# A gated spectral and token-MLP mixer: row block 0 normalised one row group at a time, its w1 rows loaded alone on both queues, seven w1 column blocks in the first group, and the unfolding of the inverse transform in pairs

## The chip, the cores and the metric

The kernel runs on one core of one Trainium2 chip. The time is device microseconds of one launch. The kernel before took 135.03 us (median of three runs: 133.51, 135.03 and 135.1). Everything else below comes from one profiled execution of it, whose span, from the first to the last instruction, is 132.6 us.

## The reference, cut to what matters

S = 2048 rows (positions), D = 512 columns, F = 1792 hidden units, bf16 in and out.

```
x = A_x                                       # (1, 2048, 512)
g = sigmoid((x * gate_w).sum(-1))             # one gate per row
X = rfft2(x) ; X = X * (w_r + i w_i)          # spectral branch, over both axes
a = irfft2(X)
h = layernorm(x over D)                       # MLP branch, no affine part
u = gelu(h^T w1 + b1)                         # contraction over the 2048 rows -> (D, F)
b = (u w2 + b2)^T                             # back to (2048, D)
out = g * a + (1 - g) * b
```

## The kernel before, in words

**How the work is cut.** Row s of the 2048 is written s = 512 q + 4 p + r: p is the partition (128 of them), q and r run from 0 to 3. A *row block* is one r; it has four *row groups* (q), each 128 x 512. The index j = 4 q + r names one of the 16 tiles of x and of h. The hidden units come in 14 column blocks `ft` of 128.

**The MLP branch.** `m1(ft, j)` (L651-657) is one matmul, 128 x 128 by 128 x 512, that adds tile j of h into the PSUM tile of block ft; 14 x 16 = 224 of them. The first NF = 6 blocks are accumulated side by side, row block after row block, while x still arrives (L659-660); their weights are tile `wa`. The other eight blocks follow one after the other, from two `wb` tiles of four blocks. A block's last matmul is followed by its gelu on ACT (L670). `m2` (L932) is the second MLP matmul, 14 per output tile j, 224 tiles' worth in all, some of the last row tile in three parts.

**The spectral branch** is a hand-made 2-D transform with four matmul stages and butterflies between them. Stage A (`fa`, L513-516) takes a row block of x after a radix-4 step on DVE (`q4a`, `q4b`, L494-501): four groups (dq = 0 to 3) of four matmuls for each r, each group evicted from PSUM by ACT into `X` (L519). Stage B (L621-624) makes `B`, evicted by ACT (L628); then the product with the spectral weights, stage I1 (L838-845), the fold `fq` into the two z tiles (L873-874), and stage I3 (L913-917). I3's result is scaled by the gate on ACT into an `eo` buffer (L923), *unfolded* on DVE (`fold`, L937-941: one copy and four additions or subtractions of 128 x 256), and added to the scaled MLP tile (`fin`, L958). Output tiles 14 and 15 (LATE) are unfolded straight into the output and get the MLP part last (L970).

**Layernorm.** For a group of two j: mean and variance on DVE (`bn`, L462-463), a square root on ACT (`sq`, L472), reciprocal and minus mean over deviation on DVE (`rec`, L476-477), then h, on DVE for j = 0, 8 and 4 (L480) and on ACT for the other 13 (L486).

**PSUM.** Eight banks under three names: `acc` 4, `fa` 2, `fb` 2. Blocks 0 to 3 of the first group accumulate in `acc`, blocks 4 and 5 in `fb`. Stage A uses `fa`, so it has two banks that turn.

**What sets the order.** Nothing is ordered by hand. Each piece of work is a task with an engine, an estimated duration, dependencies, a priority and the pools it takes and gives back (`add`, L149). `Plan.order` (L170-233) plays all tasks through a list scheduler and emits them in the order of its start times; the engines then run their streams in exactly this order and wait where a result is not there. So an estimate that is changed changes the order, and a wait of one instruction holds up all that stand behind it on its engine. Loads go out on the SP queue (L303), some of the first on the ACT queue as well. `wa` and `wb` later hold w2.

**Start of the kernel.** The four x tiles of row block 0 are asked for first, two on each queue; then table `ta` for r = 0 (the moving operand of stage A), and the w1 rows of row block 0 in two loads of 384 KB (L381-383), one on each queue; then x, `ta` and w1 of row blocks 1, 2 and 3 on SP. PE runs 13 warm-up matmuls on zeros (L353).

Of the kernel before, what the change touches and what calls it, by code (L numbers as in the profile page):

```python
# [16 lines left out]
P = 128  # L17
# [5 lines left out]
NW = 7  # L23
# [108 lines left out]

class Task:
# [3 lines left out]
class Plan:  # L137
# [32 lines left out]
    def order(self):  # L170
# [16 lines left out]
        while events:  # L187
# [16 lines left out]
            while progress:  # L204
                progress = False
                for eng, ts in pending.items():
# [15 lines left out]
                    if best.nbytes:  # L222
                        dma_free = max(dma_free, now + best.dur + 1.0) + best.nbytes / 350e3
                        end = dma_free + 0.4
                        clock[eng] = max(clock[eng], dma_free - 5.0)
# [36 lines left out]
def kernel(  # L262
# [25 lines left out]
    NEO, NES = 4, 2  # L288
# [65 lines left out]
    NWARM = 13  # L354
# [4 lines left out]
    add("ACT", 1.5, presq, reads=["eps"], writes=["omg"], prio=-5)  # L359


    for r in range(4):
        if r == 0:
            for q in range(4):
                ld([("x", 0, q)], lambda q=q: t["x"][:, q, 0, :], x4[:, q, 0, :], 131072, -9 + 0.1 * q, "SP" if q < 2 else "ACT")
        else:
            ld([("x", r, q) for q in range(4)], lambda r=r: t["x"][:, :, r, :], x4[:, :, r, :], 524288, 2 * r)
        ld([("ta", r)], lambda r=r: t["ta"][:, r, :], tabs["ta"][:, r, :], 163840, 2 * r + 0.2)

    NF = 6  # L370
# [3 lines left out]
    def ld_w1(r, qs=slice(0, 4), eng=None):  # L374
        def emit():
            if "wa" not in t:
                t["wa"] = sb([P, 4, 4, FA], BF16, "wa")
            dma(t["wa"][:, qs, r, :], w1v[:, qs, r, 0:FA], eng)
        return emit

    for b in range(2):  # L381
        add(("SP", "ACT")[b], 0.5, ld_w1(0, slice(b, 4, 2), (None, A)[b]), writes=[("w1", 0, 4 * b), ("w1", 0, 4 * b + 8)], prio=(0.5, -4)[b],
            alloc=() if b else ["wa"], nbytes=393216, after=[a0])
    for r in range(1, 4):
        add("SP", 0.5, ld_w1(r), writes=[("w1", 0, 4 * q + r) for q in range(4)], prio=2 * r + 0.5, nbytes=786432)
# [8 lines left out]
    def ld_wb(k, q):  # L394
        def emit():
            dma(t["wb", k][:, q], w1v[:, q, :, FA + D * k:FA + D * (k + 1)])
        return emit
# [6 lines left out]
    def load_wb(k, after=(wba, wbb)):  # L404
        for q in range(4):
            add("SP", 0.5, ld_wb(k, q), writes=[("w1", k + 1, 4 * q + r) for r in range(4)], prio=10 + 12 * k + 0.1 * q,
                nbytes=524288, after=after)
# [38 lines left out]
    HACT = set(range(NJ)) - {0, 8, 4}  # L446
    for r in range(4):
        xk = [("x", r, q) for q in range(4)]
        groups = [[0, 2], [1, 3]] if r == 0 else [[0, 1], [2, 3]]
        t["xf", r] = None  # L450
        for b, qs in enumerate(groups):
# [4 lines left out]
            def colv(name, qs=qs, r=r):  # L456
                v = t[name][:].rearrange("p (q r) -> p q r", r=4)
                return v[:, qs[0]:qs[-1] + 1:qs[1] - qs[0], r]

            for j in js:  # L460
# [3 lines left out]
                add("DVE", d1(512) + 0.12, bn, reads=[("x", r, j // 4)], writes=[("mv", j)], prio=1.2 * r - (0.6 if j in (0, 8) else 0))  # L464
            mvk = [("mv", j) for j in js]

            def mvv(c, qs=qs, r=r):
                v = t["mv"][:].rearrange("p (q r) c -> p q r c", r=4)
                return v[:, qs[0]:qs[-1] + 1:qs[1] - qs[0], r, c]
# [13 lines left out]
            add("DVE", 0.25 + 0.32 * len(own), rec, reads=xb + mvk, writes=[("rstd", *g)] + [("h", j) for j in own], prio=1.2 * r - 0.2)  # L483
# [18 lines left out]
        if r == 0:  # L502
            add("DVE", 2 * tt(1024) + 2 * tt(512), lambda: (q4a(0), q4b(0)), reads=xk, writes=[("xf", 0), "st"], prio=-0.5, alloc=["xf"])
# [142 lines left out]
    jorder = [4 * q + r for r in range(4) for q in ((0, 2, 1, 3) if r == 0 else range(4))]  # L646

    def w1of(ft):
        return 0 if ft < NF else 1 + (ft - NF) // 4

    def m1(ft, j):  # L651
        if j == jorder[0]:
            t["u", ft] = ps([P, D], F32, "fb" if 4 <= ft < NF else "acc", 2 if 4 <= ft < NF else 4)
        k = w1of(ft)
        w, c = (t["wa"], ft) if k == 0 else (t["wb", k - 1], (ft - NF) % 4)
# [8 lines left out]
    for n, (ft, j) in enumerate(order):  # L664
        last = j == jorder[-1]
        bank = "fb" if 4 <= ft < NF else "acc"
        m1t.append(add("PE", mm(512), lambda ft=ft, j=j: m1(ft, j), reads=[("w1", w1of(ft), j), ("h", j)], writes=[("u", ft)],
# [209 lines left out]

    for i in range(NW):
        n = (0, 3, 5)
        if i in n:  # L880
            k = n.index(i)

            def w2alloc(k=k):
                t["w2", k] = sb([P, 6, S], BF16, "wa") if k == 0 else sb([P, 4, S], BF16, "wb", 2)
            add("SP", 0.01, w2alloc, writes=[("w2a", k)], prio=31 + i, alloc=["wa" if k == 0 else "wb"])

        def ldw2(i=i):
            w, o = w2at(2 * i)
            dma(w[:, o:o + 2, :], w2v[:, 2 * i:2 * i + 2, :])
        add("SP", 0.5, ldw2, reads=[("w2a", k)], writes=[("w2", i)], prio=31 + i, nbytes=1048576)  # L890

    def w2at(ft):
        k = w1of(ft)
        return t["w2", k], ft - (0, NF, NF + 4)[k]
# [8 lines left out]
    for grp in groups:  # L903
        for j in grp:
# [13 lines left out]
            if j % 2 == 0:  # L918
                add("PE", mm(*[129] * 10), i3, reads=[("z", 0), ("z", 1), "tg"], writes=[("i3", j), ("i3", j + 1)], prio=4, alloc=["fa", "fb"])

            def i3ev(j=j):
                t["eo", j] = sb([P, 2, L], BF16, "eo", NEO)
                A.activation(t["eo", j][:], t["i3", j][:], ActF.Copy, scale=t["g"][:, j:j + 1])  # L923
            add("ACT", act(512, 1), i3ev, reads=[("i3", j), "g"], writes=[("eo", j)], prio=1.5, alloc=["eo"], free=[tag])
            parts = [slice(0, D)] if j < NJ - 1 else [slice(0, L), slice(L, L + P), slice(L + P, D)]
            for n, cs in enumerate(parts):
                for ft in range(NFT):
# [6 lines left out]
                    add("PE", mm(cs.stop - cs.start), m2, reads=[("w2", ft // 2), ("gl", ft)], writes=[("y", j, n)], prio=20 + j + 0.3 * n,  # L934
                        alloc=[("acc", "fa", "fb")[n]] if ft == 0 else (), after=m1t[-16:-15] if ft == 0 else ())
            def fold(e, o, s):
                V.tensor_copy(s[:, :, :, 0], e[:, :, 0:129:128].rearrange("p h k -> p k h"))  # L937
                V.tensor_add(s[:, 0, :, 1:P], e[:, :, 1:P], e[:, :, P + 1:L])
                V.tensor_sub(s[:, 1, :, P - 1:0:-1], e[:, :, 1:P], e[:, :, P + 1:L])
                V.tensor_add(o[:, 0:4:3], s[:, :, 0], s[:, :, 1])  # L940
                V.tensor_sub(o[:, 2:0:-1], s[:, :, 0], s[:, :, 1])
            tfold = tiny(1) + 4 * tt(256)
            quart = lambda v: v.rearrange("p h (k d) -> p (h k) d", k=2)

            if j < LATE:
                def es(j=j, fold=fold, quart=quart):
                    s = sb([P, 2, 2, P], BF16, "es", NES)
                    fold(t["eo", j], quart(t["eo", j][:]), s)
                add("DVE", tfold, es, reads=[], writes=[("eo", j)], prio=4, alloc=["es"], free=["es"])

# [4 lines left out]

                def fin(j=j):
                    o = tbuf(j)
                    V.tensor_add(o, o, t["eo", j][:])  # L958
                add("DVE", tt(512), fin, reads=[("eo", j)], writes=[("o", j)], prio=4, free=["eo"])
            else:  # L960
                def es(j=j, fold=fold, quart=quart):
                    e, s = t["eo", j], sb([P, 2, 2, P], BF16, "es", NES)
                    V.tensor_scalar_add(e[:, 0, 0:129], e[:, 0, 0:129], t["ombb2"][:, j:j + 1])
                    fold(e, quart(tbuf(j)), s)
# [50 lines left out]
```

## Time and profile before

| | |
|---|---|
| median of three runs | 135.03 us |
| lowest, highest | 133.51, 135.1 us |
| span of the profiled execution | 132.6 us |
| PE / DVE / ACT busy in it | 124.6 / 115.3 / 80.5 us |
| moved by DMA | 23.18 MB, mean 175 GB/s |
| first matmul that is not warm-up | 7.71 us |
| last instruction's end on DVE (L970) | 130.09 us |

The page of the profile gives the span of the profiled execution and no launch time of its own; the span is 0.9 us below the lowest of the three runs shown and 2.4 us below their median. A matmul's end in the profile is modelled: a matmul of 512 columns is shown as 380 ns long, though the next starts 216 ns after it, so a PE that is shown busy may still have lost time. "Idle before" is the time for which an engine stood still before an instruction, with what ended it.

### The profile page before, as it was taken

Reading aid. Unit: us, or ns where it says so; the run is one execution under the profiler, and the core shown is the slowest. Engines: PE = TensorE matmul, PEld = TensorE weight load, DVE = VectorE, ACT = ScalarE, POOL = GpSimd, SP = SyncE. Lnnn points to the kernel's source line nnn. Section 1 sums busy time; section 2 is a strip of 40 time slices with the busy share of each in tenths; the row PEclk is TensorE's granted clock in tenths of the full one; section 3 lists DMA queues with packets and bytes.
Section 4 is the critical chain, followed back from the end, with each engine's and each line's share of the span. In section 5 each row is a group of like instructions: output and inputs, shape, how many; then the busy total and the mean of one; then the engine's idle time right before and its main releaser. Section 6 shows DMA issues by size and latency. Waiting matters only on the chain.

```text
span 132.6 us, 2193 instructions
## 1 busy us (share of the span) xinstructions
PE 124.6 (94%) x769; PEld 70.7 (53%) x783; DVE 115.3 (87%) x295; ACT 80.5 (61%) x155; POOL 0.2 (0%) x4
## 2 busy tenths in 40 slices
PE   6749999999999999999999999999999999999991
PEld 2234464545544566744445544556865766655590
DVE  2987999999999997389999999999598599999841
ACT  4036699999999999972222016235994857755200
POOL 0000000000000000000000000000000000000000
PEclk9999999999999999999999999999999999999999
DMA  4899999925499565999964930000000003034031
GB/s 133 245 370 394 393 380 371 321 60 134 90 309 342 96 134 131 337 373 413 421 253 72 420 146 2 0 2 5 0 0 0 5 0 158 23 135 161 2 119 40
DMA packets 17350, 23.18 MB, mean 175 GB/s; under 512 B 1446, under 2 KB 14780, under 8 KB 17340
## 3 DMA queue, kind: packets, MB, share of 16 engines
q1 hardware_dynamic: 16780, 22.39, 49.8%
q10 hardware_dynamic: 560, 0.66, 1.6%
q8 instruction: 6, 0.10, 0.3%
q14 instruction: 4, 0.03, 0.1%
HBM read 20.93 MB, written 2.10 MB: 174 GB/s over the span
## 4 chain that ended last, share of the span: by engine, by line
PE 80%; DVE 10%; DMA 6%; SPq 1%; issue 1%
PE acc L932 35%; PE acc L656 25%; DMA x<-in_A_x_dram 6%; DVE stats L462 4%; PE fb L656 3%; PE fa L838 1%; PE fb L838 1%; PE fa L624 1%; PE fb L624 1%; SPq L303 1%; DVE mv L463 1%; DVE gl L495 1%; DVE st L494 1%; PE fa L513 1%; DVE nmr L477 1%
## 5 line engine op out<-in xcount | busy, mean ns | idle before, releaser
L932 PE MATMUL acc<-gl,wb 128*128 128x512 bf16 (+1 forms) x123 | 30.5, 373 | 0.3
L656 PE MATMUL acc<-h,wb 128*128 128x512 bf16 x124 | 28.8, 379 | 0.2
L932 PE MATMUL acc<-gl,wa 128*128 128x512 bf16 (+1 forms) x94 | 23.2, 372 | 0.1
L932 PEld LDWEIGHTS <-wb 128*128 128x128 bf16 x144 | 14.9, 114 | 10.7 <-DMA wb<-in_B_w_dram 0.6
L952 ACT ACTIVATE x<-acc,ombb,omg 128x512 bf16<-128x512 f32 x14 | 10.7, 778 | 15.5 <-PE acc L932 15.4
L656 PEld LDWEIGHTS <-wb 128*128 128x128 bf16 x128 | 12.4, 97 | 13.5
L656 PE MATMUL acc<-h,wa 128*128 128x512 bf16 x62 | 16.8, 379 | 1.2 <-DVE stats L462 0.7
L932 PEld LDWEIGHTS <-wa 128*128 128x128 bf16 x108 | 11.7, 114 | 8.5
L656 PEld LDWEIGHTS <-wa 128*128 128x128 bf16 x96 | 9.1, 98 | 10.3 <-DMA wa<-in_B_w_dram 0.9
L670 ACT ACTIVATE gl<-acc,b1f 128x512 bf16<-128x512 f32 x12 | 8.5, 708 | 9.6 <-PE acc L656 9.6
L462 DVE BATCH_NORM_STATS2 stats<-x 128x6 f32<-128x512 bf16 x16 | 10.8, 673 | 2.8 <-DMA x<-in_A_x_dram 2.8
L519 ACT CAST X<-fa 128x512 bf16<-128x512 f32 x16 | 8.8, 583 | 3.9 <-PE fa L516 3.8
L486 ACT ACTIVATE h<-x,nmr,rstd 128x512 bf16<-128x512 bf16 x13 | 9.8, 805 | 1.2 <-DVE nmr L477 1.2
L684 ACT ACTIVATE x<-x 128x512 bf16<-128x512 bf16 x16 | 10.2, 672 | 0.0
L923 ACT ACTIVATE eo<-fa,g 128x512 bf16<-128x512 f32 x8 | 5.5, 688 | 6.7 <-DVE x L958 5.0
L656 PE MATMUL fb<-h,wa 128*128 128x512 bf16 x31 | 9.0, 379 | 0.0
L513 PE MATMUL fa<-rot,gl 128*128 128x256 bf16 x16 | 4.3, 272 | 2.1 <-DMA rot<-dft_ta 2.1
L353 PE MATMUL fa<-xp 128*128 128x512 bf16 x13 | 4.4, 514 | 1.2 <-DVE xp L314 1.2
L923 ACT ACTIVATE eo<-fb,g 128x512 bf16<-128x512 f32 x8 | 5.5, 686 | 0.0
L958 DVE TENSOR_TENSOR x<-x,eo 128x512 bf16<-128x512 bf16 x14 | 5.4, 418 | 0.0
L628 ACT CAST B<-fb 128x512 bf16<-128x512 f32 x8 | 5.2, 651 | 0.0
L628 ACT CAST B<-fa 128x512 bf16<-128x512 f32 x8 | 5.1, 639 | 0.0
(170 smaller groups left out, 227.3 us busy)
## 6 DMA issues: line engine op xcount, KB each, us to landing
wb<-in_B_w_dram SPq DMA_DIRECT2D x8, 512.0 KB
wb<-in_B_w_dram SPq DMA_DIRECT2D x4, 1024.0 KB
wa<-in_B_w_dram SPq DMA_DIRECT2D x3, 1024.0 KB
wa<-in_B_w_dram SPq DMA_DIRECT2D x3, 768.0 KB
x<-in_A_x_dram SPq DMA_DIRECT2D x3, 512.0 KB
out_dram<-x SPq DMA_DIRECT2D x3, 512.0 KB
rot<-dft_ti SPq DMA_DIRECT2D x1, 736.5 KB
rot<-dft_ta SPq DMA_DIRECT2D x4, 160.0 KB
```

Source lines behind the costliest of these rows:

```text
L462: V.bn_stats(out=t["stats"][:, j, :], in_=t["x"][:, j // 4, j % 4, :])
L486: add("ACT", act(512, 2), lambda j=j: A.activation(t["h"][:, j // 4, j % 4, :], t["x"][:, j // 4, j % 4, :], ActF.Identity, bias=t["nmr"][ ...
L513: T.matmul(pa[:, 1], lhsT=w(2), rhs=ta[:, 256:512], start=True, stop=False)
L519: add("ACT", act(512), lambda r=r, dq=dq: A.copy(t["X"][:, :, r, :, dq, :], t["pa", r, dq][:]), reads=[("pa", r, dq)], writes=[("X", r, dq ...
L628: A.copy(t["B"][:, lt, e, 2 * c:2 * c + 2, :].rearrange("p s (i b) -> p s i b", b=4), t["pb", lt, e, c][:].rearrange("p s b i -> p s i b"))
L656: T.matmul(t["u", ft][:], lhsT=w[:, j // 4, j % 4, c * P:(c + 1) * P], rhs=t["h"][:, j // 4, j % 4, :], start=(j == jorder[0]), stop=(j == ...
L670: gelus.append(add("ACT", act(512, 1), lambda ft=ft: A.activation(t["gl"][:, ft, :], t["u", ft][:], ActF.Gelu_apprx_tanh, bias=t["b1f"][:, ...
L684: A.activation(t["x"][:, q, r, :], t["x"][:, q, r, :], ActF.Copy, accum_out=t["glog"][:, 4 * q + r:4 * q + r + 1])
L923: A.activation(t["eo", j][:], t["i3", j][:], ActF.Copy, scale=t["g"][:, j:j + 1])
L932: T.matmul(t["y", j, n][:, cs], lhsT=w[:, o, 512 * q + r:512 * q + 512:4], rhs=t["gl"][:, ft, cs], start=(ft == 0), stop=(ft == NFT - 1))
L952: A.activation(tbuf(j).rearrange("p h d -> p (h d)"), t["y", j, 0][:], ActF.Identity, bias=t["ombb2"][:, j:j + 1], scale=t["omg"][:, j:j + 1])
L958: V.tensor_add(o, o, t["eo", j][:])
```

## The change

Four things are changed, and the planner's estimates with them, so that nearly every engine's order moves.

1. *Row block 0.* It is normalised in four groups of one j (order q = 0, 2, 1, 3) in place of two groups of two, `rec` gets an earlier and the radix-4 step a later place on DVE (PQ0 = 1.1 in place of -0.5). The x tiles go out as q = 0, 1 on SP and 2, 3 on ACT as before. Table `ta` for r = 0 now stands behind w1.
2. *First w1 rows.* The rows of q = 0 are asked for directly behind x, the lower 64 partitions on ACT and the upper 64 on SP; then q = 2 and q = 3 on ACT, q = 1 on SP.
3. *Seven column blocks first.* NF is 7: block 6 of the first group accumulates in an `fa` bank. The two `wb` tiles now get four and three blocks. w2 is loaded in 14 loads of 512 KB in place of 7 of 1 MB. Warm-up matmuls: 10 in place of 13.
4. *Unfolding in pairs.* Tiles j and j + 1 share one `eo` buffer (two buffers of a pair in place of four single ones) and are unfolded by one copy and four operations of twice the size; `fin` too runs on a pair.

```diff
-                        dma_free = max(dma_free, now + best.dur + 1.0) + best.nbytes / 350e3
-                        end = dma_free + 0.4
+                        dma_free = max(dma_free, now + best.dur + 1.0) + best.nbytes / RATE(dma_free)
+                        end = dma_free + 0.9
...
+RATE = lambda t: 300e3 if t < 2.6 else 225e3 if t < 5.9 else 380e3
...
-    NEO, NES = 4, 2
+    NEO, NES = 2, 1
...
-    NWARM = 13
+    NWARM = 10
...
-    add("ACT", 1.5, presq, reads=["eps"], writes=["omg"], prio=-5)
+    add("ACT", 0.05, presq, reads=["eps"], writes=["omg"], prio=-5)
+    Q0 = (0, 2, 1, 3)
...
-        ld([("ta", r)], lambda r=r: t["ta"][:, r, :], tabs["ta"][:, r, :], 163840, 2 * r + 0.2)
+        ld([("ta", r)], lambda r=r: t["ta"][:, r, :], tabs["ta"][:, r, :], 163840, 2 * r + 0.2 if r else -3.5)
-    NF = 6
+    NF = 7
+    WB = (0, NF, NF + 4, NFT)
...
-    for b in range(2):
-        add(("SP", "ACT")[b], 0.5, ld_w1(0, slice(b, 4, 2), (None, A)[b]), ...
+    w1_0(0, 0, LO, "ACT", -8)
+    w1_0(1, 0, HI, "SP", -8)
+    w1_0(0, 2, ALL, "ACT", -4)
+    w1_0(0, 1, ALL, "SP", -4)
+    w1_0(0, 3, ALL, "ACT", -3)
...
-        groups = [[0, 2], [1, 3]] if r == 0 else [[0, 1], [2, 3]]
+        groups = [[q] for q in Q0] if r == 0 else [[0, 1], [2, 3]]
...
+    def bankof(ft):
+        return "acc" if ft < 4 or ft >= NF else "fb" if ft < 6 else "fa"
...
-    for i in range(NW):
-        n = (0, 3, 5)
+    for i in range(NFT):
+        if i in WB:
...
-            dma(w[:, o:o + 2, :], w2v[:, 2 * i:2 * i + 2, :])
+            dma(w[:, o, :], w2v[:, i, :])
...
+                    V.tensor_copy(s[:, :, :, :, 0], e[:, :, :, 0:129:128].rearrange("p j h k -> p j k h"))
+                    V.tensor_add(s[:, :, 0, :, 1:P], e[:, :, :, 1:P], e[:, :, :, P + 1:L])
+                    V.tensor_sub(s[:, :, 1, :, P - 1:0:-1], e[:, :, :, 1:P], e[:, :, :, P + 1:L])
+                    V.tensor_add(o[:, :, 0:4:3], s[:, :, :, 0], s[:, :, :, 1])
+                    V.tensor_sub(o[:, :, 2:0:-1], s[:, :, :, 0], s[:, :, :, 1])
...
+                if j % 2:
+                    def fin(j=j):
+                        o = t["tb_"][:, j - 1:j + 1]
+                        V.tensor_add(o, o, t["eo", j // 2][:])
```

The order that results around the start, engine by engine: DVE does `bn` for q = 0 and 2, then `rec` and h of each, `bn` for q = 1 and 3, `rec` and h of q = 1, `rec` of q = 3, the whole radix-4 step of r = 0, and then four `bn` of row block 1 before its first `rec`. ACT does four square roots, h of q = 3, two stage A evictions, a square root, a third eviction, a square root, h of row block 1 for q = 0 and 1, the fourth eviction, and so on, one or two h between two evictions; its gelu table is loaded after the first eviction of row block 3. PE does 18 m1, a stage A group, 3 m1, a group, 3 m1, a group, 3 m1, a group, 8 m1, a group, and goes on so: the 16 groups of stage A stand singly, with 3 to 9 m1 between two of them.

## The prediction

> **What bounds the kernel now.** I read the page first, then the chain of waits, the timelines of PE, ACT and DVE, and the busy times by stretch. The page says that PE is the bound nearly everywhere, with DVE close to it.
>
> ```profile
> PE 124.6 (94%) x769; PEld 70.7 (53%) x783; DVE 115.3 (87%) x295; ACT 80.5 (61%) x155; POOL 0.2 (0%) x4
> PE 80%; DVE 10%; DMA 6%; SPq 1%; issue 1%
> ```
>
> The second line is the chain that ended last: PE for 80%, and before that DVE (the layernorm of x, 10%) and the load of x. Since a shown matmul overlaps the next one, I count PE by issue instead: a run of nine 512-column matmuls starts one every 0.215 us, a stage A group takes 0.33. All matmuls after the warm-up make 118.6 us, before and after the change alike (224 m1, 224 m2 and 22 us of transform). I call *lost* the clock minus the matmul work issued so far. The timeline of PE gives it at five points:
>
> ```profile
> 7.71 0.27 PE L513 MATMUL fa<-rot,gl 128*128 128x256 bf16 x1 [2.06 <-DMA rot<-dft_ta]
> ...
> 29.37 2.10 PE L656 MATMUL acc<-h,wa 128*128 128x512 bf16 x9
> ...
> 35.83 0.38 PE L706 MATMUL fa<-wt,flip 128*128 128x256 bf16 x2
> ...
> 90.62 0.22 PE L842 MATMUL fa<-rot,B 128*128 128x129 bf16 x1
> ...
> 102.92 0.22 PE L913 MATMUL fa<-tg,xp 128*128 128x129 bf16 x1
> ```
>
> 7.7 is lost at the start, 9.9 at 35.83 (work 25.9), 10.5 at 90.62 (80.1), 10.8 at 102.92 (92.1), 10.9 at PE's end, 129.7. So the start costs 7.7 us, the first 28 us another 2.2, all the rest 1.0. From PE's end to the span's it is 2.9, which the change leaves alone. What the start waits for is in the waits and the timelines of DVE and ACT:
>
> ```profile
> PE fa L513 <- DMA rot<-dft_ta: 2.1, 1, 2.1
> DVE stats L462 <- DMA x<-in_A_x_dram: 2.8, 2, 1.6
> ```
> ```profile
> 10.64 0.69 DVE L462 BATCH_NORM_STATS2 stats<-x 128x6 f32<-128x512 bf16 x1 [1.19 <-DMA x<-in_A_x_dram]
> ```
> ```profile
> 10.02 1.13 ACT L519 CAST X<-fa 128x512 bf16<-128x512 f32 x2 [0.71 <-PE fa L516]
> ...
> 26.18 3.12 ACT L486 ACTIVATE h<-x,nmr,rstd 128x512 bf16<-128x512 bf16 x4
> 29.32 1.28 ACT L670 ACT_TABLE_LOAD   x1
> ```
>
> Row block 1 of x is at DVE at 10.64, and DVE has no idle gap from there to 51 us. ACT, too, is full from 24.3 to 45.4 (20.8 of 21.1 us busy).
>
> **The start.** x is asked for as before, so `bn` begins at 3.35. With 0.81 for each `bn` (3.35, 4.17, 4.97), 0.27 for a `rec` (6.84 to 7.11) and 0.37 for an h, h of q = 0 is ready at 5.65, of q = 2 at 6.25, of q = 1 at 8.43, of q = 3 (on ACT) at 9.5; the radix-4 step (1.87, from 4.97 to 6.84) ends at 10.5. The first w1 rows: ahead of and with them are 0.75 MB, moved by 4.8 us in before's half-microsecond stretches; x of row block 0 was usable about 0.5 after its bytes, x of row block 1 about 2.0 after (1.99 MB by 8.65, landed 10.64). Bounds 5.65 (h) and 9.26 (first m1 before), I take 6.3, nearest to these two rows. So 1.4 us of the 7.7 goes.
>
> The clock: 13 warm-ups end at 5.65, seven at 0.43 us and the rest at 0.216; ten end at 5.0. The gap to the first m1 is then 1.3 us. Before it is 2.06, and 256-column matmuls follow it 0.11 apart, full speed: cost 0. The Trainium skill (TensorE: Matmul & The Clock Gate, Part 1) has the clock halved after an idle window of about 3.4 us; by that rule a first m1 after 8.4 would come cold. The trace, whose gap is shorter, cannot show it.
>
> **Row block 1 is what is late next.** x of row block 1 now has 2.13 MB up to its end in both queues together, before 1.99; at 385 GB/s (the 8.0 to 9.5 stretches) it lands 0.35 later, at 11.0. Counted by SP's own bytes alone (1.29 against 1.34 MB) it would be 10.5; a late share gives 11.4. I take 11.0, as both queues' bytes fit the landing before. The Trainium skill says the same (DMA: Bandwidth & Descriptors, Queues, rings and completion order): the queues share the same 16 engines, packet by packet. That speaks against a gain from asking on both queues; the sum does not use it.
>
> DVE now does four `bn` before the first `rec`: 11.0 + 3.24 + 0.35 = 14.55; h on ACT takes 0.80; PE has row block 1 at 15.5. By then it has done row block 0 (28 m1, four A groups) and one m1, 7.4 us of work: lost 8.1. Before it was 9.1 at that amount of work (16.86). So far the change gains 1.0, and an arrival of w1 anywhere between 5.7 and 7 gives the same.
>
> **One bank for stage A.** Block 6 holds one `fa` bank, so each A group waits for the eviction of the one before. In the trace the eviction starts 0.53 us after its group (9.49 and 10.02), lasts 0.55, and PE has the bank 0.05 later: 1.13, of which the group covers 0.33, so 3.7 m1 must lie between and ACT must be free. But ACT has one or two h (0.74 each) and a square root (0.22) between two evictions. Walking the three streams in their order: group 1 of row block 1 waits 0.3, group 2 0.2, in row block 2 groups 0, 1 and 3 wait 0.05, 0.2 and 0.2, the bias 0.2: 1.1 in all. Row block 3's first group comes at 31.65, lost 9.2. The bounds are 0, if ACT is always ahead, and 2.5, if one h more stands before each of the three longest.
>
> **The table load.** ACT's order has the gelu table (1.28) and a gelu (0.6) between row block 3's first two evictions. Eviction 0: 32.2 to 32.7; load to 34.0; gelu to 34.6; eviction 1 to 35.15. PE has five m1 (1.1 us) after its second group, ends them at 34.2 and stands 1.0 us until 35.2. Before, the load lay behind the last h, beside 29 m1. The remaining waits of row block 3, with a gate sum (0.75) ahead of an eviction, are 0.6. The first flip of W comes at 38.95 with 28.1 us of work done: lost 10.9, against 9.9 before. Here the early start is more than eaten. The load and these waits may cost 0 (table earlier, ACT ahead) to 2.5.
>
> **The middle.** ACT then has five gelu, two W evictions and nine gate sums before the first eviction of B: 38.9 + 9.4 = 48.3, before 46.41. The last B eviction moves from 56.6 to about 59.0 and with it DVE's chain: z, ready at 102.68 before, at about 105.1. PE comes to I3 with 94.0 us of work and 11.2 lost: 105.2. So PE still sets the time, by a hair. The 14 w2 loads take seven SP issues more (0.45 each); SP waits 12.8 us for PE there, so nothing; three blocks instead of four behind the last m1 may save the 0.1 lost between 70.3 and 81.4.
>
> **The pairs.** A pair of tiles takes DVE 2.69 us before (106.81 to 109.50). Twice the size, from rows of that shape (128x508 and 128x512 0.42, starts 0.335 apart; 128x1024 0.69, 0.60 apart): 0.08 + 4 x 0.335 + 0.12 + 0.60 = 2.14; eight pairs save 4.4 us of DVE. But only two pair buffers turn: the third and fifth unfolding wait for two evictions (0.57 + 0.69) after a `fin`, less the next `fin`, about 0.8 each; the last one waits about 1.4, the first 0.6 for its second tile. From z to the last unfolding: 22.3, before 22.9. DVE was 1.0 us ahead of PE at tile 14 (125.62 and 126.65), so either way nothing on the path. If the waits vanished: still nothing, PE sets the end; if they doubled, 1 us.
>
> **Sum.** Start -1.4; row block 1 +0.4; bank +1.1 where before lost 0.7; table and row block 3 +1.6 where before lost 0.2; later the same 1.0 as before: lost 11.9 against 10.9. Span 133.6 against 132.6, and on the median of 135.03 about 136.0.
>
> **Rivals.** *The early start is kept.* If ACT is ahead when PE needs it, what was gained by 15.5 us stays, and only before's own later losses (1.8 from 16.86 on) are added: lost 9.4 to 9.9, 1.0 to 1.5 us less, 133.6. For it: ACT has gaps before 16.3 in before. Against it: it has none from 24.3 to 45.4. With x of row block 1 at 10.5 and no wait in row block 3, 2.5 us or more, under 132.5. *The spectral chain sets the end* (slower). ACT's lag at the first B eviction is 1.9 in my sum; from there on each us goes through B, T and z into I3, where PE's order is fixed. With 2 us more (for instance the gate sums in front of row block 3's evictions twice) z is at 107.2, PE waits at I3, 138.0. It decides from z later than 105.2. *Cold clock*: w1 after 8.4, eight m1 at half speed, 1.7 us, and the A groups pushed behind h of row block 1: 137.5. Against it: the first w1 was there by 9.26 with twice the bytes ahead.
>
> **How the numbers follow.** My sum 0.47, early start kept 0.28, spectral chain 0.20, cold clock 0.05. A measurement of this kernel can tell about 2% (2.7 us) from no change. Faster than 132.3 is only the far end of the first rival: 0.08. Slower than 137.7 is most of the second, part of the cold clock and a tail of my sum: 0.18. Within: 0.74. The range 133.2 to 138.0 leaves out about one in ten on each side. As both signs hold much of the chance: the likeliest case alone runs from 135.0 to 137.0.
>
> **What would show it.** The first m1 near 6.3; `stats` of row block 1 near 11.0; row block 1's first m1 near 15.5 with PE idle before it; PE idle before A groups with ACT named as releaser; a gap of 1 us near 34 behind the table load; the first B eviction near 48; DVE waiting for `eo` in the unfolding. I am wrong if PE has no idle time between 16 and 39, or if z comes before 103.

## The result and the profile after

The changed kernel takes 135.88 us (median of four runs: 135.25, 135.73, 136.03, 136.06) where the kernel before took 134.64 in the runs beside it: ratio 1.011, 95% interval 1.0067 to 1.0154. So it is about 1.2 us slower, inside the 2% that were called "within". About 136.0 was forecast. The profiled execution took 135.25 us with a span of 133.1, so it is 0.6 under the median. Below, medians take in all executions of a kernel, while ratios and intervals leave out the few that took over 1.5% longer than its fastest, and the one profile of such an execution (139.29 us, the changed kernel again) is not used.

The lines of before's page about busy time and the chain of waits have these counterparts on the page after:

```profile
PE 125.3 (94%) x766; PEld 70.6 (53%) x780; DVE 112.4 (84%) x252; ACT 80.4 (60%) x157; POOL 0.2 (0%) x4
```
```profile
DVE 53%; PE 26%; ACT 13%; issue 4%; DMA 2%; DVEq 0%; ACTq 0%
```

PE is as busy as it was, but the chain that ended last no longer runs along PE: 53% of it is on DVE. The chain goes to whichever engine came last, so this alone does not say that DVE sets the time. The PE timeline after (columns: start, length, engine and line, operation, shapes, count, idle time before and what ended it) gives the places that the forecast named:

```profile
6.61 1.02 PE L670 MATMUL acc<-h,wa 128*128 128x512 bf16 x4 [1.04 <-DMA wa<-in_B_w_dram]
...
12.82 0.27 PE L524 MATMUL fa<-rot,gl 128*128 128x256 bf16 x1
...
34.67 0.27 PE L524 MATMUL fa<-rot,gl 128*128 128x256 bf16 x1 [0.91 <-ACT X L530]
...
46.30 0.38 PE L720 MATMUL fa<-wt,flip 128*128 128x256 bf16 x2
...
94.77 0.23 PE L856 MATMUL fb<-rot,B 128*128 128x128 bf16 x1 [0.22 <-DVE B L579]
...
105.12 0.22 PE L926 MATMUL fa<-tg,xp 128*128 128x129 bf16 x1
```

PE's first matmul on data starts 1.1 us earlier than before (7.71), and the first m1 2.7 us earlier (9.26). At 34.67 PE stands for ACT: that is the gap behind the table load. The third flip of W, which stood at 49.20 before, comes at 46.30. At 94.77 a matmul of stage I1 waits for a column butterfly of DVE, and at 105.12 I3 starts. The ACT timeline after shows why PE stood at 34.67:

```profile
31.56 0.58 ACT L530 CAST X<-fa 128x512 bf16<-128x512 f32 x1 [1.61 <-PE fa L527]
32.16 1.28 ACT L684 ACT_TABLE_LOAD   x1
33.46 0.69 ACT L684 ACTIVATE gl<-acc,b1f 128x512 bf16<-128x512 f32 x1
34.04 0.58 ACT L530 CAST X<-fa 128x512 bf16<-128x512 f32 x1
```

Between row block 3's first two evictions stand the load and a gelu: 2.48 us from one CAST to the next. PE has one bank, and gets it 0.05 us after the second CAST.

**Where the time went.** The table below adds up, stage by stage, what PE lost. For each matmul this is the time from its start to the next start, less columns/2400 us and 0.002 us; that is the spacing of an undisturbed run (0.216 us for 512 columns, 0.056 for 128). What is left under 0.012 us is not counted, and a gap of exactly one further 512-column matmul is taken for a missing record. The first column is the start of row block 1's first m1, and "rest" the span less this moment. The losses are counted from row block 1's last A group to the first group of stage B, from there to I3, and from I3 to PE's end.

```
                       row block 1's   rest   lost, row blocks   lost in stage   lost
                       first m1               2 and 3 to B       B and to I3     from I3
before                 16.42 (*)      116.2        0.75              0.95         0.04
pairs only             16.3 (*)       116.5        0.75              0.92         0.46
after                  14.88          118.2        2.33              1.17         0.47
  first gelu held      16.97          117.9        2.31              0.88         0.46
  gate sums held       15.92          118.2        2.44              1.00         0.46
  three pair buffers   15.17          118.1        2.33              1.16         0.32
  13 warm-ups          15.82          118.0        2.04              1.18         0.47
  W imaginary first    14.92          118.2        2.45              0.75         0.45
  gelu + gates held    15.69          118.4        2.64              0.95         0.47
  the same, planned    15.33          118.5        2.80              0.94         0.47
(*) the moment at which as much matmul work (7.35 us) was done
```

The start gained 1.5 us in this execution and the rest became 2.0 longer. Of the 2.2 us more that PE lost in the rest, 1.6 lie in row blocks 2 and 3, 0.2 in stage B to I3 and 0.4 from I3 on. The seven profiles whose kernels emit the same start (leaving out 13 warm-ups, moved w1 loads and six column blocks) put row block 1's first m1 between 14.88 and 16.97, median 15.33. So the typical gain is near 1.1 and, with the median rest of 118.2, the net loss near 0.9 by the profiles, where the launches show 1.2 to 1.6; what makes the difference is not shown. The remarkable column is "rest": it stays at 117.9 to 118.5 whichever stall was taken away. It does so because the three losses together hardly fall (3.97 us in the changed kernel, 3.65 to 4.21 in the rows below it): a stall that an edit took from PE came back at another place on PE.

### The profile page after: what moved, and what is told of

Read it like the earlier page. It is cut to its first block, busy times and chain, and to the rows that moved or that the text cites. A ratio compares the mean times of both kernels' runs of the same rounds, so it can differ in the third digit from the quotient of the medians.

```text
span 133.1 us, 2156 instructions
## 1 busy us (share of the span) xinstructions
PE 125.3 (94%) x766; PEld 70.6 (53%) x780; DVE 112.4 (84%) x252; ACT 80.4 (60%) x157; POOL 0.2 (0%) x4
## 4 chain that ended last, share of the span: by engine, by line
DVE 53%; PE 26%; ACT 13%; issue 4%; DMA 2%; DVEq 0%; ACTq 0%
PE acc L966 12%; DVE stats L473 7%; PE acc L670 4%; DVE xp L791 3%; DVE st L791 3%; ACT x L698 3%; ACT eo L937 3%; DVE st L564 3%; DVE mv L474 2%; DMA x<-in_A_x_dram 2%; ACT gl L684 2%; DVE xp L796 2%; DVE xp L563 2%; DVE B L803 2%; DVE xp L797 2%
## 5 line engine op out<-in xcount | busy, mean ns | idle before, releaser
L966 PE MATMUL acc<-gl,wa 128*128 128x512 bf16 (+1 forms) x107 | 26.9, 372 | 0.2
L966 PE MATMUL acc<-gl,wb 128*128 128x512 bf16 (+1 forms) x110 | 27.1, 372 | 0.1
L670 PE MATMUL acc<-h,wb 128*128 128x512 bf16 x108 | 25.7, 379 | 0.2
L966 PEld LDWEIGHTS <-wa 128*128 128x128 bf16 x126 | 13.4, 114 | 9.8 <-issue 0.2
L966 PEld LDWEIGHTS <-wb 128*128 128x128 bf16 x126 | 13.4, 114 | 9.4
L670 PEld LDWEIGHTS <-wb 128*128 128x128 bf16 x112 | 10.9, 98 | 11.7
L670 PEld LDWEIGHTS <-wa 128*128 128x128 bf16 x112 | 10.1, 98 | 10.7 <-DMA wa<-in_B_w_dram 1.8
L530 ACT CAST X<-fa 128x512 bf16<-128x512 f32 x16 | 9.3, 578 | 5.1 <-PE fa L527 5.1
L684 ACT ACTIVATE gl<-acc,b1f 128x512 bf16<-128x512 f32 x11 | 7.6, 694 | 7.8 <-PE acc L670 7.7
L670 PE MATMUL fa<-h,wa 128*128 128x512 bf16 x15 | 5.4, 379 | 0.0
L483 ACT ACTIVATE rstd<-mv,eps 128x2 f32<-128x2 f32 (+1 forms) x10 | 3.0, 295 | 3.4 <-DVE mv L474 2.8
```

The costliest lines, as they stand in the source:

```text
L530: add("ACT", act(512), lambda r=r, dq=dq: A.copy(t["X"][:, :, r, :, dq, :], t["pa", r, dq][:]), reads=[("pa", r, dq)], writes=[("X", r, dq ...
L670: T.matmul(t["u", ft][:], lhsT=w[:, j // 4, j % 4, c * P:(c + 1) * P], rhs=t["h"][:, j // 4, j % 4, :], start=(j == jorder[0]), stop=(j == ...
L684: gelus.append(add("ACT", act(512, 1), lambda ft=ft: A.activation(t["gl"][:, ft, :], t["u", ft][:], ActF.Gelu_apprx_tanh, bias=t["b1f"][:, ...
L966: T.matmul(t["y", j, n][:, cs], lhsT=w[:, o, 512 * q + r:512 * q + 512:4], rhs=t["gl"][:, ft, cs], start=(ft == 0), stop=(ft == NFT - 1))
```

## The experiments

The theory: what the start gains is spent again at the single `fa` bank and the gelu table load in row blocks 2 and 3; without these the gain would be seen. The rivals: ACT's lag at stage B goes through the spectral chain (DVE) to the end; the pairs cost something; the first rows or the cold clock spoil the start. Each run stands beside runs of the kernel before on the same chip (its medians there: 134.40 to 134.66).

### The changed kernel again

No edit.

> The changed kernel unchanged, as the measure for the other kernels of this call. Every theory: 1.011 times the kernel before, and in the trace the same 8.6 us lost (clock minus matmul work) at row block 3's first stage A group, 9.9 at the first flip of W, 10.5 at I1, 11.1 at I3 and about 11.6 at the end of PE.

Measured: 136.23, ratio 1.0114 [1.0073, 1.0156]. The loss is confirmed.

### Pairs alone

The kernel before with the unfolding of the changed kernel and nothing else of it:

```diff
-    NEO, NES = 4, 2
+    NEO, NES = 2, 1
...
+                    o = e if j < LATE else (tbuf(j), t["tb_"][:, j - 1:j + 1])[1]
...
-                    V.tensor_add(o, o, t["eo", j][:])
+                        V.tensor_add(o, o, t["eo", j // 2][:])
```

> The kernel before with nothing but the unfolding in pairs, two pair buffers. Theory 1: DVE is 3 to 4 us less busy, waits for the evictions into the pair buffers appear, and PE sets the end as before: within 0.3 us of the kernel before. Theory C (the pairs cost it): 0.8 to 1.4 us more than the kernel before. If the unfolding had been on the path: 0.5 us or more less.

Measured: 134.56 beside 134.55, ratio 1.0018 [0.9987, 1.005]: no change that can be told. PE loses 0.4 more from I3 on (0.46 for 0.04), the same as in the changed kernel; the interval, which reaches up to 0.7 us, leaves open whether this gets into the time. The larger part of the loss of the whole change lies elsewhere.

### Three pair buffers

```diff
-    NEO, NES = 2, 1
+    NEO, NES = 3, 1
```

> The changed kernel with three pair buffers of the unfolding in place of two. Theory 1: DVE's waits for the evictions into them (2.0, 0.8, 0.8, 1.1 us) shrink, the unfolding ends some 2 us earlier, PE is less often held up at I3; up to 0.3 us less, as the end is set by PE's matmuls. Theory 2 (the pair buffers cost what was gained): 0.8 to 1.2 us less. Theory 3 (late spectral chain): nothing.

Measured: 136.02, ratio 1.0099 [1.0064, 1.0133], as without the edit. The waits of DVE for `eo`, from the list of waits (waiting engine and line, releaser: total, times, longest), after and with three buffers:

```profile
DVE es L949 <- ACT eo L937: 3.6, 3, 2.0
```
```profile
DVE es L949 <- ACT eo L937: 2.0, 1, 2.0
```

Two of the three waits are gone, 1.6 us, and the time stays. These waits are not on the path to any extent that shows, as forecast.

### Two fa banks, six column blocks

```diff
-    NF = 7
+    NF = 6
-        return "acc" if ft < 4 or ft >= NF else "fb" if ft < 6 else "fa"
+        return "fb" if 4 <= ft < NF else "acc"
```

> The changed kernel with six column blocks in the first group, as before the change, so that stage A has two banks; early start and pairs stay. Theory 1 (one bank and the table load between two evictions take the start's gain back): PE has 0.86 us less work before row block 1, so about 8.4 us are lost there, but the stall of 0.9 us at 34 and the smaller ones are gone: 9.2 lost at 31 and 9.4 at the first flip of W, 0.3 to 0.7 us less than the changed kernel. Theory B (late loads and clock in the start): w1 rows are a seventh smaller and come 0.2 us earlier, so 0.1 to 0.3 us less. Theory C (pairs): the same as the changed kernel.

Measured: 142.06, ratio 1.0553 [1.0493, 1.0613]. In row blocks 2 and 3 up to the first flip PE lost 0.77 us, nearly as the kernel before does (0.64), where the changed kernel loses 2.24. These 1.5 us are not the second bank's alone, though: with this edit the planner also puts the table load ahead of row block 3's evictions, as it was in the kernel before (29.32 there). The time was lost later, to another thing. The planner put DVE's first piece of work on the imaginary W ahead of the second radix-4 step of the half transform. The load on ACT's timeline, then DVE's and PE's:

```profile
28.65 1.28 ACT L684 ACT_TABLE_LOAD   x1
```
```profile
52.41 0.42 DVE L740 TENSOR_SCALAR W<-W 1x1028 bf16<-1x1028 bf16 x1 [6.36 <-ACT x L698]
```
```profile
59.04 0.29 PE L632 MATMUL fa<-tb,X 128*128 128x128 bf16 x1 [4.88 <-DVE X L614]
```

DVE stands 6.36 us and PE behind it 4.88, after 1.26 at the third flip. The profile names a copy of ACT for the first; but the last of the twelve DMAs that bring the imaginary W was issued only from 50.42 to 50.99, so the load is what was late. This prices an order that rests on a landing which the planner puts too early. What the second bank is worth in time, the run cannot show.

### First gelu held back

The first gelu, which brings the table load, may only come after the last eviction of stage A:

```diff
-            add("ACT", act(512), lambda r=r, dq=dq: A.copy(t["X"][:, :, r, :, dq, :], t["pa", r, dq][:]),
+            aev = add("ACT", act(512), lambda r=r, dq=dq: A.copy(t["X"][:, :, r, :, dq, :], t["pa", r, dq][:]),
...
-                free=[bank]))
+                free=[bank], after=[aev]))
```

> The changed kernel, but the first gelu, and with it the load of ACT's gelu table, may come only after the last eviction of stage A. Theory 1 (the early start is worth 1.1 us until 31 us, and the single bank with the table load between two evictions of row block 3 takes it back before 38 us): the idle 0.9 us of PE near 34 goes, the first flip of W comes with about 9.2 us lost where it was 9.9, and the time falls by 0.4 to 0.8 us against the changed kernel. Theory 2 (the pair buffers of the unfolding cost what was gained): the stall near 34 goes too, but it comes back as waiting elsewhere, time the same within 0.3 us. Theory 3 (the ACT backlog of gate sums makes the spectral chain late, and that sets the end): z as late as before or later, since the gelu are now behind the evictions; time the same or up to 0.5 us more.

Measured: 136.18, ratio 1.0113 [1.007, 1.0155]: no gain. Row block 3's loss up to the first flip fell from 1.36 to 0.43 as the theory wanted, and the wait came back at the second flip of W, whose `fb` bank ACT must first empty with a gelu. ACT and PE with the gelu held:

```profile
38.00 1.28 ACT L684 ACT_TABLE_LOAD   x1
39.29 2.42 ACT L684 ACTIVATE gl<-acc,b1f 128x512 bf16<-128x512 f32 x4
41.59 1.28 ACT L684 ACTIVATE gl<-fb,b1f 128x512 bf16<-128x512 f32 x2
```
```profile
7.10 1.89 PE L670 MATMUL acc<-h,wa 128*128 128x512 bf16 x4 [1.44 <-DVE mv L474]
8.78 1.06 PE L670 MATMUL fb<-h,wa 128*128 128x512 bf16 x2
...
42.34 0.38 PE L720 MATMUL fb<-wt,flip 128*128 128x256 bf16 x2 [1.12 <-ACT gl L684]
```

The load was moved, its 1.28 us of ACT were not. The first lines show a second thing: here the first four m1 took 1.89 us in place of 1.02. The full clock had not come: eight m1 started 0.36 to 0.43 apart, which cost 1.6 us, and row block 1 began at 16.97. That is a matter of this execution, not of the edit: the start is emitted as in the changed kernel.

### Gate sums held back

```diff
-            gates.append(add("ACT", act(512) + 0.1, ga, reads=xk, writes=[("xg", q, r)], prio=5))
+            gates.append(add("ACT", act(512) + 0.1, ga, reads=xk, writes=[("xg", q, r)], prio=5, after=[pl.last_w["B", 1, 3]]))
```

> The changed kernel, but the 16 gate sums on ACT come only after the last eviction of stage B. Theory 1: the first eviction of B comes at about the time of the first B group's end, near 47 as now, since PE starts B at 46.5; the later ones come without gate sums between; z 1 to 2 us earlier than 104.9; the 0.6 us lost between I3 and the end of PE go, the 9.9 at the first flip stay: 0.3 to 0.7 us less. Theory 2 (pair buffers): z comes earlier, but the evictions into the pair buffers still wait, time the same within 0.3 us. Theory 3 (the late spectral chain alone costs it): z below 103 and the whole 1 us against the kernel before comes back.

Measured: 136.2, ratio 1.0117 [1.0078, 1.0156]: no gain. Row block 3's loss stayed (1.26 for 1.36), so it is the load and not the gate sums. The loss from the first flip to B's first group rose from 0.09 to 0.59, at the third flip. That it waited there for the imaginary W is likely but not shown: the profile names PE itself, while it names that load in the profile of the kernel with both held and the load in the plan (below). And the start shows how the lateness of the first rows goes on. PE with the gate sums held:

```profile
6.88 1.02 PE L670 MATMUL acc<-h,wa 128*128 128x512 bf16 x4 [1.36 <-DMA wa<-in_B_w_dram]
...
9.14 1.04 PE L670 MATMUL acc<-h,wa 128*128 128x512 bf16 x4 [0.59 <-DMA wa<-in_B_w_dram]
...
13.86 0.27 PE L524 MATMUL fa<-rot,gl 128*128 128x256 bf16 x1
...
15.92 0.81 PE L670 MATMUL acc<-h,wa 128*128 128x512 bf16 x3 [0.41 <-ACT h L497]
```

and ACT in the changed kernel:

```profile
13.35 0.58 ACT L530 CAST X<-fa 128x512 bf16<-128x512 f32 x1 [0.38 <-PE fa L527]
13.83 0.30 ACT L483 ACTIVATE rstd<-mv,eps 128x2 f32<-128x2 f32 x1
14.03 1.51 ACT L497 ACTIVATE h<-x,nmr,rstd 128x512 bf16<-128x512 bf16 x2
```

ACT's order is: evict row block 0's third A group, square root, h of row block 1. So, where PE is the later one, row block 1's first m1 comes a fixed time after that A group: 12.82 and 14.88 after, 13.86 and 15.92 here, 14.91 and 16.97 with the gelu held, 13.63 and 15.69 with both held, 13.27 and 15.33 with the load in the plan (both below); 2.06 each time. Where DVE is the later one it is more: 2.22 with three pair buffers and 2.23 with the imaginary W first, where DVE's last mean and variance (14.02, 13.77) end just before ACT's square root. In the changed kernel's own profile DVE has what h needs at 13.96, 0.07 before ACT's h begins: the two just meet, and each tenth by which PE's third A group is later than there goes around through ACT to row block 1.

### Both held back

The last two diffs together.

> The changed kernel with both edits that did nothing alone: the first gelu and the table load only after the last eviction of stage A, and the 16 gate sums only after the last eviction of stage B. Theory 1 (ACT as a whole is too full between 14 and 48 us, so that PE waits for it somewhere whatever is moved): alone, the table's stall of 1.25 us only moved to the second flip of W, 1.29 us, because gelu and gate sums stood there; with the gate sums gone too both go, the stalls of PE from row block 1 on fall from 3.9 to 2.7 us, and the time by 0.8 to 1.2 us against the changed kernel. Rival (something else holds stage B, the late W or DVE): stalls shift to stage B, time within 0.3 us of the changed kernel.

Measured: 136.17, ratio 1.0151 [1.0109, 1.0194]. Without gate sums ahead of it the second flip still waits for ACT: 1.32 us, now at 40.53. On ACT and on PE:

```profile
36.18 1.28 ACT L684 ACT_TABLE_LOAD   x1
37.48 2.42 ACT L684 ACTIVATE gl<-acc,b1f 128x512 bf16<-128x512 f32 x4
39.77 1.28 ACT L684 ACTIVATE gl<-fb,b1f 128x512 bf16<-128x512 f32 x2
```
```profile
40.53 0.38 PE L720 MATMUL fb<-wt,flip 128*128 128x256 bf16 x2 [1.32 <-ACT gl L684]
```

The load's 1.28 us stand ahead of the gelu that PE waits for, so without them nearly all of the wait would be gone.

### Both held back, and the load in the plan

The last kernel, and the planner counts the load with the first gelu:

```diff
-            gelus.append(add("ACT", act(512, 1), lambda ft=ft: A.activation(
+            gelus.append(add("ACT", act(512, 1) + (0 if gelus else 1.28), lambda ft=ft: A.activation(
```

> The kernel of e10_tg (first gelu after stage A, gate sums after stage B) with one estimate changed: the planner now counts 1.28 us for the gelu table with the first gelu. On PE this only moves the second flip of W six matmuls back, 1.3 us, behind four matmuls of block 7; DVE's order is the same, ACT's changes by one place. In e10_tg PE stood 1.3 us at that flip for a gelu. Theory 1, as mended (the table load costs PE 1.3 us wherever PE's fixed order reaches a bank that ACT has not emptied; behind work that needs no such bank it costs nothing): the stall at the second flip falls below 0.2 us, the stalls of PE from row block 1 on fall from about 3.9 to 2.4 us, and the time is 1.0 to 1.3 us less than the changed kernel's, about 135.0, still 0.3 to 0.6 us above the kernel before. Rival (ACT as a whole is the bound until stage B, whatever PE's order): the stall comes back at block 7 or in stage B, and the time is within 0.3 us of the changed kernel's.

Measured: 135.59, ratio 1.0069 [1.0041, 1.0096]; the interval meets that of the changed kernel. PE's order changed, where six matmuls go ahead of the second flip, and ACT's by one place. Its PE timeline:

```profile
40.36 0.38 PE L720 MATMUL fb<-wt,flip 128*128 128x256 bf16 x2
...
47.23 0.38 PE L720 MATMUL fa<-wt,flip 128*128 128x256 bf16 x2 [1.09 <-DMA wt<-in_A_w_i_dram]
```

The wait for the load is gone, and PE stands 1.09 for the imaginary W instead: it is the next in the line. With it, what was lost up to B is no less (2.80 us, where it was 2.64 without the load in the plan).

### Imaginary W first

Its loads ahead of the second `wb` tile's:

```diff
-        add("SP", 9.0 - 2 * comp, ld_W(comp), writes=[("W", comp), ("wt", comp)], prio=17 + 8 * comp, nbytes=300000, after=[a0])
+        add("SP", 9.0 - 2 * comp, ld_W(comp), writes=[("W", comp), ("wt", comp)], prio=17 + comp, nbytes=300000, after=[a0])
```

> The changed kernel with the imaginary part of the spectral weights W loaded ahead of the second wb tile in place of behind it. The change put the third flip of W at 46.3, where it stood at 49.1 before, and in one run it stood 2.3 us there for the load. Theory A (clock): the same within 0.3 us. Theory B (W lands too late now in many executions): no wait at the third flip, the spread shrinks, the median falls by 0.3 to 0.8 us. Theory C (the pairs cost it): the same.

Measured: 136.34, ratio 1.0139 [1.0089, 1.0188]. The third flip moved to 44.20 and waits for nothing; stage B and I1 lose 0.75 instead of 1.17. But the loss in row block 3 (1.36), with the table load's stall in it, stands, and the "rest" is 118.2 as ever. This edit and the one above were not tried together.

### Thirteen warm-ups

```diff
-    NWARM = 10
+    NWARM = 13
```

> The changed kernel with 13 warm-up matmuls again in place of 10. In the runs so far its first matmul with data started between 6.33 and 7.10, and in one of them (7.10) nine matmuls then went one every 0.43 us, half speed, until 10.3, in another the first one and a half. Theory A (ten warm-ups do not always bring the full clock, and the time of the changed kernel is more than its best profile shows because of that): with 13 the first matmuls go every 0.216 us in the profile, the median falls by 0.3 to 0.7 us and the spread shrinks. Theory B (what varies is when the w1 rows and W land; the clock is a side show): within 0.2 us of the changed kernel. Theory C (the pairs cost it): the same.

Measured: 135.82, ratio 1.0094 [1.0056, 1.0133], not to be told from the changed kernel. m1 runs 0.216 apart from its first on, and begins at 6.76 with DVE named as the releaser. In its one profile row block 1 comes at 15.82, no earlier than the others. Of the seven profiles with the same start, two show matmuls at half rate behind the warm-ups (1.6 and 0.3 us). So a late clock is not what costs the 1.2 us in the median.

### w1 rows earlier on the ACT queue

The rows of q = 2 and 3 asked for before ACT's square-root table load:

```diff
-    w1_0(0, 2, ALL, "ACT", -4)
+    w1_0(0, 2, ALL, "ACT", -6)
-    w1_0(0, 3, ALL, "ACT", -3)
+    w1_0(0, 3, ALL, "ACT", -5.5)
```

> The changed kernel with the w1 rows of q = 2 and q = 3 asked for on ACT's queue ahead of the load of ACT's square root table, at about 2.2 and 2.7 us in place of 3.3 and 4.3. Theory 2 (the early start is worth less in most executions than in the best profile, because these rows come late: PE stood 0.6 us for them in two of the profiles): no wait for wa after the first matmul, row block 1's first matmul at 14.9 or before, median 0.3 to 0.8 us less. Rival (the same bytes now go in front of x of row block 1 and of the rows of q = 0, which come later by as much): first matmul 0.3 to 0.6 us later, no gain.

Measured: 135.67, ratio 1.0113 [1.0077, 1.0149]. The waits for `wa` are gone, and another took their place. ACT's timeline with this edit:

```profile
1.66 2.35 ACTq L305 DMA_DIRECT2D wa<-in_B_w_dram  x3
4.03 1.28 ACT L360 ACT_TABLE_LOAD   x1 [4.03 <-DMA x<-in_A_x_dram]
5.53 0.47 ACT L483 ACTIVATE rstd<-mv,eps 128x1 f32<-128x1 f32 x2
```

Three issues hold ACT's stream for 2.35 us, so the table load comes at 4.03 (2.22 in the changed kernel) and the first square root at 5.53 (4.59); the first m1 waits for h until 7.13, and row block 1 comes at 15.78.

### All together

Gelu and gate sums held, w1 rows earlier, 13 warm-ups, three pair buffers.

> All of it together: table load after stage A, gate sums after stage B, w1 rows asked for ahead of the square root table, 13 warm-ups, three pair buffers. If both theories hold: start 0.5 us and later stalls 1.2 us better than the changed kernel, about 134.2, 0.3 us less than the kernel before. If only the first holds: 135.0, level with the kernel before. If neither: 136.

Measured: 136.37, ratio 1.0187 [1.014, 1.0235]: no better than any part. In its profile PE again waits 1.3 us for a gelu at the second flip. The stalls do not add up like separate causes; they lie in one tight order in which each removed wait uncovers the next.

## Why the forecast was right, point by point

**What stands.** The places are those of the forecast: the start is earlier, and more than its gain is lost at the one bank and around the table load. "Lost 11.9 against 10.9", 1.0 more: in the profile PE's last matmul starts 0.7 us later (130.16 for 129.48), and the launches show 1.2 to 1.6. First m1: 6.3 forecast, 6.61 seen, and 6.17 to 7.13 over all runs. Row block 1's first m1: 15.5, seen 14.88 here and 15.33 as the median of seven profiles. The one bank: 1.1 from row block 1's to row block 3's first A group where before lost 0.7, seen 1.21 for 0.80; with the second bank 0.80. z: 105.1, seen 104.86. I3: 105.2, seen 105.12. What the sums of PE's lost time do not give is a proof by experiment: no run took these losses away and got the time back.

**Mis-sized.** Five terms.

- "x of row block 1 at 11.0". DVE begins it at 10.42 with no wait; until then it is busy with the radix-4 step, so the landing is at most 10.42. The DVE timeline after:

```profile
10.42 0.69 DVE L473 BATCH_NORM_STATS2 stats<-x 128x6 f32<-128x512 bf16 x1
...
13.63 0.14 DVE L487 RECIPROCAL rstd<-rstd 128x2 f32<-128x2 f32 x1
13.80 0.16 DVE L488 SCALAR_TENSOR_TENSOR nmr<-mv,rstd 128x2 f32<-128x2 f32 x1
...
38.00 0.69 DVE L537 TENSOR_TENSOR st<-X 128x1024 bf16<-128x1024 bf16 x1 [1.12 <-ACT X L530]
...
57.91 0.18 DVE L754 CAST c<-B 128x8 f32<-128x8 bf16 x1 [3.37 <-ACT B L639]
```

- "An arrival of w1 anywhere between 5.7 and 7 gives the same". This step failed. DVE's `rec` for row block 1 is done at 13.96, but ACT takes h only after an eviction that waits for PE, and PE's A group stands behind the m1 of row block 0. Once that A group starts later than the 12.82 of this profile, whether by a late first m1, a later wait for `wa` or a late clock, its lateness passes on one to one (2.06 us from A group to m1 in five profiles), unless DVE is later still.
- "Cost 0" of the clock. It was 0 in five of the seven profiles, 0.3 us in one and 1.6 in another.
- "Table and row block 3 +1.6 where before lost 0.2", seen 1.45 for 0.28 up to the first B group, and the middle came 0.6 to 0.9 earlier than forecast (first flip 38.02 for 38.95, first B eviction 47.39 for 48.3, last 58.37 for 59.0).
- "Eight pairs save 4.4 us of DVE". With the pairs alone DVE's busy time fell by 3.4 us (115.3 to 111.9).

Two sums are off by a little: 11.0 + 3.24 + 0.35 is 14.59, not 14.55, and 129.7 less 118.6 is 11.1, not 10.9. Neither moves the forecast.

**What was missing.** "Later the same 1.0 as before". From the first B group on PE lost 1.64, before 0.99: nothing more in stage B, 0.23 more in I1, where it now waits for DVE's butterflies, and 0.43 more from I3 on, of which the pairs alone make 0.42. This made good what the start and the table load had left over. The errors of single terms, up to about 0.6 us, cancelled; that the sum came within 0.2 us of the median is luck.

**The rivals.** *The early start is kept* did not happen: in row blocks 2 and 3 ACT waits for PE at one moment (1.61 before 31.56) and PE for ACT at the next, and PE loses 2.24 us up to the first flip. *The spectral chain sets the end* "decides from z later than 105.2", and z came at 104.86: not passed, but with 0.3 us to spare. DVE waits 1.12 for `X` at 38.00 and 3.37 for the last `B` until 57.91 (2.18 before); from there it is nearly full until I1, where it waits for ACT three times (0.76, 0.69 and 0.91). *Cold clock*: shown once in full size (eight m1 at half speed were priced at 1.7 us, and eight cost 1.6), but through a clock that came late after the warm-ups, not through a late w1.

**Why no edit helped.** What PE lost from row block 2 on was 3.97 us in the changed kernel and 3.65 to 4.21 in the profiles with edits. Each stall that went came back at PE's next wait, for a gelu at the second flip or for the imaginary W at the third. That PE and DVE are tied further on, so that taking away a stall on PE alone would give DVE's end, fits z, which is ready 0.3 us before PE's I3, and PE's wait for `B` in I1. It was not shown by an experiment that frees both. Also open: the imaginary W earlier with the load in the plan; row block 0's third eviction moved behind the first h; two `fa` banks with DVE's work on the imaginary W left behind the butterflies; and the early start without the other changes. None of these was tried.

## What to carry to other kernels

An earlier start on one engine is worth what the next engine in the loop can take: follow the emitted order around the loop (here A group, eviction, square root, h, m1) before counting a late load as hidden. When a pool goes from two buffers to one, walk the engine that empties it through its own order, with the costs that the plan does not hold, such as a table load. If a removed stall leaves the time from there to the end the same, add up the lost time stage by stage and look where it came back. Judge the start from several profiles: here row block 1 began anywhere between 14.88 and 16.97 with the same emitted start.

## What the runs showed of the hardware

**The clock at the start varies between executions of the same start.** Warm-up matmuls of 512 columns start 0.43 us apart from 1.21 us on. After ten of them matmuls came 0.216 apart from the first m1 on (6.61) in the changed kernel, from 7.07 on with three pair buffers, and from 10.42 on with the gelu held, where 1.44 us of idle time lay in between. Thirteen do not make it certain either: the spacing changed at 5.40 in the profile of that edit, but in that of all edits together only at 7.42, after all 13 and the first two m1. The Trainium skill (TensorE: Matmul & The Clock Gate, Part 1) has a window of about 3.4 us that runs freely, so that the number of cold matmuls varies from run to run; the 7.07 and 10.42 of two profiles lie 3.35 apart, which fits.

**An idle PE halves it again.** With two `fa` banks PE stood 4.88 us. The windows of that stretch (stretch, length, PE busy and count, granted clock, DMA share, GB/s):

```profile
54.00:56.00 2.00, 0.16 (x1) 1.00 1.00 340
56.00:58.00 2.00, 0.00 (x0) 0.66 0.88 316
58.00:60.00 2.00, 0.96 (x7) 0.50 1.00 395
60.00:62.00 2.00, 2.00 (x12) 0.50 1.03 414
```

The granted clock is 0.50 for the next 4 us, and the groups of stage B took 0.64 us each in place of 0.33. The Trainium skill (TensorE: Matmul & The Clock Gate, Part 1) puts the point at an idle window of about 3.4 us; 4.88 is over it, and the changed kernel's gaps of about 1 us, at which the clock stayed, are under it.

**Three DMA issues on ACT hold its stream for 2.35 us** (w1 rows earlier on the ACT queue): 0.54, 0.59 and 0.33 us each, and 0.84 us between the second and the third. That is longer than the 1.28 us of the table load that they overtook.
